# A spectral filter's weights in two buffers, loaded and stored at other places

## The chip, the cores and the metric

The kernel runs on one core of one Trainium2 chip, as one program. Its time is in device microseconds; the measure is the median of repeated runs. A profile is one more execution, recorded by the hardware: its span runs from the first to the last instruction of the program.

Five engines take part, each with its own queue, served in order: PE (TensorE, the matmuls), DVE (VectorE), ACT (ScalarE), POOL (GpSimd) and SP (SyncE, which here only issues DMAs). ACT and POOL issue a few DMAs too.

## The reference

The program computes a forward pass and all its gradients. The input x has 2048 rows of 448. Cut to what matters:

```python
def _A_ref(x, w_r, w_i):                       # w_r, w_i: 2048 x 225, the filter
    X = jnp.fft.rfft2(x.astype(jnp.float32), axes=(-2, -1))
    X = X * (w_r + 1j * w_i)
    return jnp.fft.irfft2(X, s=(S, D), axes=(-2, -1)).astype(jnp.bfloat16)

def _B_ref(x, w1, b1, w2, b2):
    h = _layernorm(x, axis=-1)
    u = _gelu(jnp.einsum("bsd,sf->bdf", h, w1) + b1)
    y = jnp.einsum("bdf,fs->bds", u, w2) + b2
    return y.transpose(0, 2, 1)

h  = x + _A_ref(_layernorm(x), w_r, w_i)
h2 = h + _B_ref(_layernorm(h), w1, b1, w2, b2)
# outputs: h2, and the gradients of x, w_r, w_i, w1, b1, w2, b2 for a given grad_out
```

The filter is read in the forward pass (X times W), read again in the backward pass (the gradient of x), and its gradient, of the same size, is an output. In bf16 the real and imaginary part are 0.92 MB each.

## The kernel before

**The transform.** The two-dimensional transform over 2048 x 448 is done as matmuls with small tables. The *first step* works by 16 tiles t of 128 rows: `row_a` multiplies a folded, normalized tile by the table `Rm` scaled with the rows' deviation, `row_b` by the table of the 448-point transform. The results of two tiles at a time are then moved by DMA to another arrangement of partitions, `D2`: these are the *row moves* (L697, at the end of `row_b`). Seven of eight go out on SP's queue, the last on ACT's. They are deferred by `RESH_LAG` in the program's order.

The *second step* (`s2_stage`, L704) takes `D2` in four sets s = 0 to 3 of four groups each: three small tables (`Vt`, `Ut`, `Un`) finish the forward transform of the set, `on_mult` multiplies by the filter on DVE, and three more tables begin the inverse transform. The result of each set is moved by DMA to `D3` (L740), by POOL, and of the last set by SP, POOL and ACT together. Then `inv_rows` (L765) finishes the inverse, tile by tile, with the row table `RTm` (made from `Rm` by one matmul in `gen_RT`, L525) and the table `csI`.

The forward pass and the backward pass both go through these steps; the backward `s2_stage` has `bwd_mult`, which multiplies by the filter's conjugate and then writes the filter's gradient over the filter, set by set.

**Work in the gaps.** PE runs other matmuls between these steps: `fill(n)` takes n pieces from a generator. In the forward pass it is `dg_gen` (L838), 14 x 16 matmuls of w2 transposed with grad_out, w2's tiles loaded by `load_w2T` (L303): the first five are turned on PE, the others come by a transposed DMA (L312). From the tenth tile on the loads are held back (`held_w2`) until the first step's end. In the backward pass `gw_gen` makes the gradients of w2 and w1, with transposed tiles from `st_load` (L1266) and `load_du` (L1252), and stores at L1372 and L1369.

**The filter.** One buffer `rW` holds it: 128 partitions, real and imaginary part (c), 16 groups (g), 225 columns. Partition 2q holds rows 16q and on in rising order, partition 2q + 1 rows in falling order, so a rising part is one run of 3600 elements in memory and a falling one is 16 runs of 225. `w_io` (L579) is a generator of 18 DMAs, either way: for each part four rising pieces of 16 partitions, four falling ones, and one for the row that is left over. `W_AT` says how many loads are issued at which tile of the first step (two at each of tiles 0 to 5, six at tile 6). The last four (rising, imaginary) go on POOL's queue, each behind a one-element memset on DVE that holds it back until DVE is there; the others go on SP's. For the gradient the same 18 moves go on SP in the last stage, at the tiles that `GW_AT` lists.

**Orders.** The instructions of PE, SP, DVE and ACT are issued in the order of the program text; POOL's are placed by a scheduler. SP's transfers take turns on eight semaphores, so each waits for the landing of the one eight before it. POOL also runs the Newton iterations (`newton_gp`, L407, lines L410 to L416) that give the deviation of each group of tiles; DVE scales `Rm` with it (`scale_R`, L621) and folds the tile (`fold_quarters`, L644) ahead of `row_a`.

The lines around the end of the first step that the change touches:

```python
    for _ in w_loads:
        pass
    ...
    turn_biases, place_biases = load_biases()
    cap[0] = NFB
    while held_w2:
        held_w2.pop(0)()
    fill(4)
    gen_RT()
    fill(7)
```

Of the kernel before, what the change touches and what calls it, by code (L numbers as in the profile page):

```python
# [17 lines left out]
P = 128  # L18
S = 2048
D = 448  # L20
DF = 225
KW = 226
# [3 lines left out]
NG = 16  # L26
# [98 lines left out]
def kernel(  # L125
# [20 lines left out]
    nc = tc.nc  # L146
# [99 lines left out]
    rS = region("rS", 7232)  # L246
    rO = region("rO", 3 * S)
    rX = region("rX", NG * 2 * KW)
    rW = region("rW", NG * 2 * KW)
    r452 = region("r452", 8 * 452)  # L250
    rAT = region("rAT", 2 * 4 * P)
    rst = region("rst", 2 * 7 * P)
# [320 lines left out]

    Wc = cut(rW, 0, 2, NG, DF)
    W = Wc.rearrange("p c g k -> p g c k")

    def w_io(dr, di, store):  # L579
        Wq = Wc.rearrange("(q s) c g k -> s q c g k", s=2)  # L580
        for c_, d in ((0, dr), (1, di)):
            moves = []
            for i in range(4):
                moves.append((Wq[0][16 * i:16 * i + 16, c_].rearrange("l g k -> l (g k)"), 16 * i, [[P * DF, 16], [1, 16 * DF]]))
                g0 = 0 if i else 1
                moves.append((Wq[1][16 * i:16 * i + 16, c_, g0:NG, :], P - 16 * i - g0,
                              [[P * DF, 16], [-DF, NG - g0], [1, DF]]))
            moves.append((Wq[1][0:16, c_, 0, :], 64, [[P * DF, 16], [1, DF]]))
            late = [m for n, m in enumerate(moves) if n in (0, 2, 4, 6)] if c_ and not store else []
            early = moves if not late else [m for n, m in enumerate(moves) if n not in (0, 2, 4, 6)]  # L590
            for n, (sb, row, dims) in enumerate(early + late):
                d_ap = bass.AP(d.tensor, d.offset + row * DF, dims)
                eng = nc.sync if n < len(early) else gp_
                if eng is gp_:
                    i = 32 * (n - len(early))
                    nc.vector.memset(Wc[i:i + 1, 1, 8, 0:1], 0.0)
                eng.dma_start(out=d_ap if store else sb, in_=sb if store else d_ap)
                yield

# [321 lines left out]
    GROUPS = {0: (6, 8), 1: (8, 10), 3: (10, 12), 5: (12, 14), 7: (14, 16)}  # L921
    STATS = {0: (6, 7), 1: (8, 9), **{t: (t + 8,) for t in range(2, 8)}}
    INV_S = {11: 0, 12: 1, 13: 2, 14: 3}
    W_AT = {**{t: 2 for t in range(6)}, 6: 6}
    FILL_A = (4, 4, 8, 12, 6, 3, 3, 4, 5, 3, 3, 2, 2, 2, 3, 3)
    FILL_B = (0, 0, 2, 2, 2, 2, 4, 4, 3, 2, 2, 2, 2, 2, 2, 2)
    def uv_step():
# [4 lines left out]
    for t in range(NT):  # L932
# [34 lines left out]
        if t in GROUPS:  # L967
            a, b = GROUPS[t]
            newton_gp(mvx[:, a:b, 1], rstd_x[:, a:b], slice(a, b))
        for _ in range(W_AT.get(t, 0)):  # L970
            next(w_loads, None)
        if t in INV_S:
# [6 lines left out]
        fill(FILL_B[t])  # L979
    for _ in uv:  # L980
        pass
    for _ in w_loads:
        pass
    gp_.memset(csF[:, 0, :, 0:1], 1.0)
    gen_inv_d(0)
    fill(6)
    gen_inv_d(1)
    turn_biases, place_biases = load_biases()
    cap[0] = NFB
    while held_w2:  # L990
        held_w2.pop(0)()
    fill(4)
    gen_RT()
    fill(7)

    def fwd_mult(s, j, x, y):
        w_mult(x, set_of(W, s)[:, 2 * j:2 * j + 2], y, False)
# [300 lines left out]

    def bwd_mult(s, j, xc, y):
        xs = set_of(Xs, s)[:, 2 * j:2 * j + 2, :, 0:DF]  # L1300
        gw = set_of(W, s)[:, 2 * j:2 * j + 2]
# [74 lines left out]
    for t in range(NT - LAG, NT + 4):  # L1376
        if t == 13:
            st_load(3)
        if t == NT - 2:
# [103 lines left out]
```

## Time and profile before

| What | Value |
|---|---|
| time, median of 3 runs | 340.99 us (340.43 to 341.34) |
| time of the profiled execution | 340.34 us |
| its span | 338.3 us |
| granted TensorE clock | 0.998 |
| first step, until the second starts | 0 to 48.4 us |
| forward second step, until `inv_rows` starts | 48.4 to 75.4 us |
| backward second step, until `inv_rows` starts | 238.7 to 288.9 us |
| last stage | 288.9 to 338.3 us |
| filter loads (L597): first to last issue | 11.5 to 37.9 us |
| filter gradient stores (L597): first to last issue | 289.2 to 320.6 us |
| row moves (L697): issue to landing, least, median, most | 2.3, 2.7, 3.7 us |
| moves behind the second step (L740): the same | 3.8, 5.5, 6.9 us |

How to read the views that follow. A *timeline* line gives start, length, engine, line, operation, what is written from what, how often, and in brackets how long the engine stood idle before it and what ended that. In the *chain of waits*, each line is start, length and what was then on the way to the end. In the view of *waits*, each line is who waited for whom, then total, times and the longest, in us. A transfer issued by SP, ACT or POOL is "DMA_DIRECT2D" or "DMA_TRANSPOSE"; SPq is SP's queue. Names of buffers are shown without their numbers, and `D2` and `D3` lie in the buffers shown as `r`. L84 is the helper through which DVE's and ACT's operations are issued; L220 and L225 are the helpers of the matmuls, L225 that of the small tables.

### The profile page before, as it was taken

What the parts mean: (1) busy time and instruction counts of PE and PEld (TensorE: products, weight loads), DVE (VectorE), ACT (ScalarE), POOL (GpSimd) and SP (SyncE); (2) the same over time, 40 slices, a digit from 0 to 9 for tenths busy, and PEclk for the clock granted to TensorE, in tenths of its full rate; (3) what the DMA queues carried; (4) which work ended last, traced back from release to release, by engine and by line L of the source; (5) the groups of instructions that cost most, each with busy time, mean ns of one, the idle gap of its engine ahead of it and who ended that gap; (6) DMA issues with size and microseconds to landing.
All of it is one profiled execution on the core that took longest, in us unless ns stands there. A gap on an engine that the chain in (4) does not pass through costs nothing.

```text
span 338.3 us, 7987 instructions
## 1 busy us (share of the span) xinstructions
PE 330.2 (98%) x2893; PEld 174.6 (52%) x2893; DVE 251.7 (74%) x670; ACT 206.7 (61%) x448; POOL 84.6 (25%) x254
## 2 busy tenths in 40 slices
PE   8999989999999999999999999999999999999995
PEld 4666554456545555555555555554344434555552
DVE  8998739827947888593227888786697993599994
ACT  6987666848965534423222346665588875588882
POOL 7767202412210000000001111210020222156670
PEclk9999999999999999999999999999999999999999
DMA  7999899959899999687877889837699999978885
GB/s 251 400 203 182 190 258 141 227 125 279 230 378 287 348 279 242 179 274 192 193 178 164 174 188 155 176 84 232 221 220 302 290 244 252 284 188 278 245 293 200
DMA packets 136198, 78.03 MB, mean 231 GB/s; under 512 B 86528, under 2 KB 127592, under 8 KB 136032
## 3 DMA queue, kind: packets, MB, share of 16 engines
q1 hardware_dynamic: 133288, 73.13, 84.5%
q0 software_dynamic: 2448, 3.83, 5.3%
q8 instruction: 22, 0.36, 0.5%
q10 hardware_dynamic: 424, 0.58, 0.5%
q14 instruction: 16, 0.13, 0.1%
HBM read 28.33 MB, written 22.04 MB: 149 GB/s over the span
## 4 chain that ended last, share of the span: by engine, by line
PE 83%; DVE 6%; DMA 4%; ACT 3%; issue 1%; POOL 1%; SPq 0%; DVEq 0%; ACTq 0%
PE ps_mm L220 68%; PE ps_ff L220 9%; PE ps_ff L225 3%; DMA r<-r 3%; ACT rO L84 2%; PE ps_mm L375 2%; DVE rS L84 2%; DVE r L84 1%; DMA r<-rX 1%; DVE rX L84 1%; DVE stats L84 1%; DVE rA L84 1%; ACT rE L84 1%; PE ps_mm L318 0%; DVE rG L84 0%
## 5 line engine op out<-in xcount | busy, mean ns | idle before, releaser
L220 PEld LDWEIGHTS <-r 128*128 128x128 bf16 (+2 forms) x628 | 58.6, 105 | 48.5 <-issue 3.0
L220 PEld LDWEIGHTS <-rS 128*128 128x128 bf16 (+1 forms) x468 | 36.2, 97 | 31.9 <-issue 6.0
L84 ACT CAST rO<-ps_mm 128x512 bf16<-128x512 f32 (+1 forms) x68 | 36.5, 584 | 14.5 <-PE ps_mm L220 11.9
L220 PE MATMUL ps_mm<-rD,r 128*128 128x448 bf16 x224 | 44.5, 352 | 0.0
L220 PEld LDWEIGHTS <-rst 128*128 128x128 bf16 (+1 forms) x320 | 23.9, 97 | 30.4 <-issue 12.1
L740 POOL DMA_DIRECT2D r<-r x29 | 17.4, 605 | 67.3 <-ACT r L84 56.7
L220 PE MATMUL ps_mm<-rC,rE 128*128 128x448 bf16 x144 | 32.1, 353 | 0.0
L220 PE MATMUL ps_mm<-rB,r 128*128 128x448 bf16 x160 | 31.2, 352 | 0.2 <-DVE rB L84 0.2
L220 PE MATMUL ps_mm<-rG,rst 128*128 128x512 bf16 (+1 forms) x128 | 28.5, 380 | 0.0
L220 PE MATMUL ps_mm<-r,rst 128*128 128x512 bf16 (+2 forms) x144 | 27.3, 345 | 0.0
L84 ACT ACTIVATE r<-ps_mm,rstd_h 128x448 bf16<-128x448 f32 x16 | 10.1, 634 | 26.8 <-PE ps_mm L220 26.8
L84 DVE SCALAR_TENSOR_TENSOR r<-ps_mm,b2col,r 128x448 bf16<-128x448 f32 x16 | 10.9, 682 | 19.9 <-PE ps_mm L220 18.6
L84 ACT ACTIVATE r<-rC 128x448 bf16<-128x448 bf16 x16 | 9.1, 570 | 26.7 <-DMA out_dram<-r 13.8
L84 ACT CAST r<-ps_ff 128x452 bf16<-128x452 f32 x43 | 23.1, 592 | 3.1 <-PE ps_ff L220 1.2
L1220 POOL TENSOR_SCALAR lcol<-lcol 128x1 f32<-128x1 f32 x16 | 8.5, 530 | 64.7 <-ACT r L84 64.7
L84 ACT ACTIVATE rG<-rG 128x896 bf16<-128x896 bf16 x14 | 13.3, 950 | 14.9 <-DVE rG L84 14.7
L220 PEld LDWEIGHTS <-rO 128*128 128x128 bf16 (+1 forms) x165 | 15.4, 98 | 12.3 <-ACT rO L84 0.2
L84 ACT CAST rS<-ps_ff 128x512 bf16<-128x512 f32 x31 | 18.0, 583 | 4.2 <-PE ps_ff L220 4.2
L220 PE MATMUL ps_ff<-csI,rAT 113*128 113x224 bf16 (+1 forms) x108 | 19.0, 298 | 0.2 <-DVE rA L84 0.2
L84 ACT CAST rG<-ps_mm 128x512 bf16<-128x512 f32 (+1 forms) x28 | 14.0, 539 | 7.6 <-PE ps_mm L220 7.5
L84 ACT CAST rAT<-ps_ff 113x512 bf16<-113x512 f32 x24 | 13.9, 586 | 7.7 <-PE ps_ff L220 7.5
L84 DVE TENSOR_SCALAR rG<-rG 128x896 bf16<-128x896 bf16 x28 | 10.9, 389 | 10.0 <-ACT rG L84 10.0
(200 smaller groups left out, 647.4 us busy)
## 6 DMA issues: line engine op xcount, KB each, us to landing
out_dram<-rO SPq DMA_DIRECT2D x34, 256.0 KB, 3.3
r<-in_B_w_dram SPq DMA_DIRECT2D x5, 1024.0 KB, 9.1
r<-r POOLq DMA_DIRECT2D x29, 113.0 KB, 5.5
out_dram<-rG SPq DMA_DIRECT2D x11, 256.0 KB, 3.1
r<-in_B_w_dram SPq DMA_DIRECT2D x3, 896.0 KB, 5.6
rS<-in_B_w_dram SPq DMA_DIRECT2D x3, 896.0 KB
rB<-in_B_w_dram SPq DMA_DIRECT2D x5, 512.0 KB, 8.1
r<-r SPq DMA_DIRECT2D x11, 226.0 KB, 2.5
```

The lines of the kernel that those rows point to most:

```text
L84: fn(**kw)
L220: nc.tensor.matmul(out, lhsT=lhsT, rhs=rhs, start=start, stop=stop)
L225: nc.tensor.matmul(out, lhsT=lhsT, rhs=rhs, start=start, stop=stop)
L375: nc.tensor.matmul(idle[:, 0:D], lhsT=rAT[:, 0:P], rhs=rAT[:, 0:D], start=True, stop=True)
L740: defer(RESH_LAG, lambda g=g, ab=ab, eng=eng: eng.dma_start(out=D3[rowbase(g):rowbase(g) + 29:4, :, :, :], in_=ab), ab)
L1220: gp_.tensor_scalar(out=m1, in0=ms, scalar1=-1.0 / D, scalar2=None, op0=ALU.mult)
```

## The change

The filter has two buffers of eight groups each, `rW[0]` for sets 0 and 1, `rW[1]` for sets 2 and 3, and `w_set(s)` picks a set. `w_io` goes through them one after the other. The four rising pieces of a part become one move of 64 partitions (4 blocks of 16 rows in memory, runs of 1800 elements); the falling pieces keep 16 partitions and have 8 groups, 7 in the piece beside the left-over row. That makes 12 moves for the first buffer and 10 for the second. On loading, the first four moves of the second buffer (falling, real) go on POOL's queue, behind one memset on DVE at tile 9.

The 12 loads of the first buffer are spread over tiles 0 to 8, POOL's four come at tile 9, and the other six are queued on SP behind the row moves: the two rising moves, then the first held w2 load, then the four falling moves, then the other held w2 loads. The loads of the biases are queued after these in the program text; in SP's order they stand behind the second held w2 load.

`gen_RT` is called behind `s2_stage` instead of ahead of it. The stores of the filter's gradient begin within the backward `s2_stage`: four after each of its passes 2, 3 and 4 (these are the first buffer's twelve), and the other ten at tiles 0 to 9 of the last stage.

```diff
-    rW = region("rW", NG * 2 * KW)
+    rW = [region(n, NG * DF) for n in ("rW0", "rW1")]
...
-    Wc = cut(rW, 0, 2, NG, DF)
-    W = Wc.rearrange("p c g k -> p g c k")
+    Wc = [cut(r, 0, 2, NG // 2, DF) for r in rW]
+
+    def w_set(s):
+        return Wc[s // 2].rearrange("p c (a b) k -> p b a c k", b=2)[:, s % 2]
 
     def w_io(dr, di, store):
-        Wq = Wc.rearrange("(q s) c g k -> s q c g k", s=2)
-        for c_, d in ((0, dr), (1, di)):
-            moves = []
-            for i in range(4):
-                moves.append((Wq[0][16 * i:16 * i + 16, c_].rearrange("l g k -> l (g k)"), 16 * i, [[P * DF, 16], [1, 16 * DF]]))
...
-            for n, (sb, row, dims) in enumerate(early + late):
+        H = NG // 2
+        for e in range(2):
+            Wq = Wc[e].rearrange("(q s) c g k -> s q c g k", s=2)
+            ups, dns = [], []
+            for c_, d in ((0, dr), (1, di)):
+                up, dn = Wq[0][:, c_], Wq[1][:, c_]
+                ups.append((d, up.rearrange("q g k -> q (g k)"), H * e, [[16 * DF, 4], [P * DF, 16], [1, H * DF]]))
+                for i in range(4):
+                    g0 = 0 if e or i else 1
+                    dns.append((d, dn[16 * i:16 * i + 16, g0:H], P - 16 * i - H * e - g0,
+                                [[P * DF, 16], [-DF, H - g0], [1, DF]]))
+                if not e:
+                    dns.append((d, dn[0:16, 0], 64, [[P * DF, 16], [1, DF]]))
+            moves = dns[:4] + ups + dns[4:] if e else ups[:1] + dns[:5] + ups[1:] + dns[5:]
+            for n, (d, sb, row, dims) in enumerate(moves):
+                eng = gp_ if e and n < 4 and not store else nc.sync
                 d_ap = bass.AP(d.tensor, d.offset + row * DF, dims)
...
-    W_AT = {**{t: 2 for t in range(6)}, 6: 6}
+    W_AT = {0: 2, 1: 1, 2: 2, 3: 1, 4: 2, **{t: 1 for t in range(5, 9)}, 9: 4}
...
+        if t == 9:
+            nc.vector.memset(Wc[1][:, 0, 0:2, 0:1], 0.0)
...
-    for _ in w_loads:
-        pass
...
-    turn_biases, place_biases = load_biases()
     cap[0] = NFB
+    for _ in range(2):
+        next(w_loads)
+    held_w2.pop(0)()
+    for _ in w_loads:
+        pass
     while held_w2:
         held_w2.pop(0)()
+    turn_biases, place_biases = load_biases()
     fill(4)
-    gen_RT()
     fill(7)
...
     s2_stage(lambda s: set_of(Xs, s), fwd_mult, 8, (8,) * 5, 0, split=True)
     sc.activation(out=warm, in_=eps_h, func=ACT.Sqrt)
+    gen_RT()
     fill(21)
...
+    g_out = w_io(out_2, out_3, True)
+
+    def store_gw(n):
+        for _ in range(n):
+            next(g_out)
...
-    s2_stage(lambda s: X_ring.next(), bwd_mult, 14, (14, 28, 14, 28, 20), N_FILL_B[4], {0: lambda: load_du(1), 1: lambda: (load_du(0), load_xall(0)), 2: lambda: load_xall(1), 3: lambda: load_du(2)},
+    s2_stage(lambda s: X_ring.next(), bwd_mult, 14, (14, 28, 14, 28, 20), N_FILL_B[4], {0: lambda: load_du(1), 1: lambda: (load_du(0), load_xall(0)), 2: lambda: (load_xall(1), store_gw(4)),
+              3: lambda: (load_du(2), store_gw(4)), 4: lambda: store_gw(4)},
              2.0 * INV_SD)
     Meter.slack = 2.0
-    g_out = w_io(out_2, out_3, True)
     X_AT = {0: 2, 4: 3}
-    GW_AT = tuple(range(12)) + tuple(range(1, 12, 2))
+    GW_AT = tuple(range(10))
```

More of the change, by code (lines that the diff above doesn't have):

```diff
@@ L572, in gen_inv_d @@
                         sc.activation(out=o, in_=i_, func=ACT.Copy, scale=f[0:KC])
-    Wc = cut(rW, 0, 2, NG, DF)
-    W = Wc.rearrange("p c g k -> p g c k")
+    Wc = [cut(r, 0, 2, NG // 2, DF) for r in rW]
+    def w_set(s):
+        return Wc[s // 2].rearrange("p c (a b) k -> p b a c k", b=2)[:, s % 2]
     def w_io(dr, di, store):
-        Wq = Wc.rearrange("(q s) c g k -> s q c g k", s=2)
-        for c_, d in ((0, dr), (1, di)):
-            moves = []
-            for i in range(4):
-                moves.append((Wq[0][16 * i:16 * i + 16, c_].rearrange("l g k -> l (g k)"), 16 * i, [[P * DF, 16], [1, 16 * DF]]))
[L585 to L590, printed above, removed]
-            for n, (sb, row, dims) in enumerate(early + late):
+        H = NG // 2
[14 more added lines that the diff above has]
+                eng = gp_ if e and n < 4 and not store else nc.sync
@@ L592, in w_io @@
                 d_ap = bass.AP(d.tensor, d.offset + row * DF, dims)
[L593 to L596, printed above, removed]
                 eng.dma_start(out=d_ap if store else sb, in_=sb if store else d_ap)
@@ L987 @@
     gen_inv_d(1)
-    turn_biases, place_biases = load_biases()
     cap[0] = NFB
+    for _ in range(2):
[3 more added lines that the diff above has]
+        pass
     while held_w2:
         held_w2.pop(0)()
+    turn_biases, place_biases = load_biases()
     fill(4)
-    gen_RT()
     fill(7)
     def fwd_mult(s, j, x, y):
-        w_mult(x, set_of(W, s)[:, 2 * j:2 * j + 2], y, False)
+        w_mult(x, w_set(s)[:, 2 * j:2 * j + 2], y, False)
     s2_stage(lambda s: set_of(Xs, s), fwd_mult, 8, (8,) * 5, 0, split=True)
     sc.activation(out=warm, in_=eps_h, func=ACT.Sqrt)
+    gen_RT()
     fill(21)
@@ L1300, in bwd_mult @@
         xs = set_of(Xs, s)[:, 2 * j:2 * j + 2, :, 0:DF]
-        gw = set_of(W, s)[:, 2 * j:2 * j + 2]
+        gw = w_set(s)[:, 2 * j:2 * j + 2]
         w_mult(xc, gw, y, True)
```

## The prediction

> **What bounds the kernel now.** I read the page first, then the waits, the timelines of the engines around every wait of TensorE, the chain of waits, and the queue of SyncE (SP).
>
> ```profile
> PE 330.2 (98%) x2893; PEld 174.6 (52%) x2893; DVE 251.7 (74%) x670; ACT 206.7 (61%) x448; POOL 84.6 (25%) x254
> ...
> DMA  7999899959899999687877889837699999978885
> ...
> q10 hardware_dynamic: 424, 0.58, 0.5%
> ```
>
> TensorE (PE) is busy 98% of the span, in program order, and the change leaves its matmuls as they are. So the change can win only what PE stands idle, and lose what it makes PE wait. The DMA row shows engines near full in most slices.
>
> ```profile
> PE ps_ff L225 <- DMA r<-rX: 0.9, 1, 0.9
> ...
> PE ps_ff L220 <- DMA r<-r: 0.7, 2, 0.5
> ...
> PE ps_ff L220 <- DVE rS L84: 0.7, 1, 0.7
> ```
>
> These are PE's largest waits behind its start: 0.91 us for a row move (L697) at the start of the second step, 0.49 and 0.24 for the moves behind the second steps (L740), 0.66 for a fold on VectorE. All PE waits after the start come to some 3.2 us, which is the ceiling of any gain. Two have causes that the diff touches. First the fold, by the timelines of POOL, DVE and PE:
>
> ```profile
> 28.34 0.20 POOL L413 TENSOR_TENSOR nt_f<-rstd_x 128x2 f32<-128x2 f32 x1
> 28.57 1.76 POOL L597 DMA_DIRECT2D rW<-in_A_w_i_dram  x3
> 30.34 0.24 POOL L414 TENSOR_TENSOR nt_f<-nt_f,mvx 128x2 f32<-128x2 f32 x1
> 30.54 0.53 POOL L597 DMA_DIRECT2D rW<-in_A_w_i_dram  x1
> ...
> 33.15 0.20 POOL L416 TENSOR_TENSOR rstd_x<-nt_f,rstd_x 128x2 f32<-128x2 f32 x1
> ```
>
> ```profile
> 33.38 0.25 DVE L84 TENSOR_SCALAR rX<-Rm,rstd_x 128x128 bf16<-128x128 bf16 x1 [0.81 <-POOL rstd_x L416]
> ...
> 36.20 0.32 DVE L84 TENSOR_SCALAR rX<-Rm,rstd_x 128x128 bf16<-128x128 bf16 x1 [0.78 <-POOL rstd_x L416]
> ```
>
> ```profile
> 35.02 0.40 PE L220 MATMUL ps_ff<-rX,rS 128*128 128x128 bf16 x4 [0.66 <-DVE rS L84]
> ```
>
> Four filter loads sit between the Newton operations on POOL and hold them for 1.76 + 0.53 = 2.29 us. DVE waits 0.81 us for the result, and PE 0.66 us for DVE. Now the start of the second step, by the chain, and SP's own timeline ahead of it:
>
> ```profile
> 43.01 1.23 DVE rX L84 x2
> 44.24 0.47 SPq L697
> 44.81 3.45 DMA r<-rX
> 48.40 0.72 PE ps_ff L225 x24
> ```
>
> ```profile
> 39.29 2.78 SPq L312 DMA_TRANSPOSE rO<-in_B_w_dram  x1
> 42.17 1.23 SPq L697 DMA_DIRECT2D r<-r  x2
> 43.50 1.85 SPq L697 DMA_DIRECT2D r<-rX  x3
> ```
>
> The last casts end at 44.24; SP, behind a long transposed load and five row moves, issues the last move only at 44.81, and it lands 3.45 us later. PE had come to the end of its fill at 48.40 - 0.91 = 47.49.
>
> **The change part by part.** Until the row moves SP issued 14 filter loads and POOL 4; now SP issues 12, of half the bytes (0.92 MB of 1.84), POOL issues 4 behind its last Newton operation, and 6 follow the last row move, with a transposed w2 load between them.
>
> *POOL.* The 2.29 us leave the Newton chain: its result at 33.35 would be there at 31.1, and DVE is ready for it at 32.57. So DVE's 0.81 go; its folds end at 34.96 - 0.81 = 34.15, before PE asks at 35.02 - 0.66 = 34.36. Gain for PE 0.66. The second wait (0.78) shrinks too and is worth the 0.06 that PE waits at 38.44. On POOL's queue the four new loads stand before a memset (needed at 43.94) and the first moves of L740 at 56.87; at 0.5 to 0.75 us each, from about 35 on, they are gone by 38. The four DVE memsets (59 ns each) become one. If the cover is gone, four loads of 0.6 us on POOL cost nobody anything before 43.9.
>
> *Row table.* One 128x128 matmul leaves the fill; the matmul behind it starts 0.05 us later now (45.94 to 45.99). Its cast (0.28 us at 47.87 on DVE) goes to ACT after the table load that ends at 72.77, and ACT is idle until 75.81; its reader starts at 75.37. Cover: 2 us of idle ACT; without it 0.3 us. Where it goes, PE has a wait of 0.49 that takes the 0.05. Gain before the step 0.05, cost 0.
>
> PE therefore reaches the end of its fill at 47.49 - 0.66 - 0.06 - 0.05 = 46.72.
>
> *Row moves.* They must have landed by then. The move on ACT's queue is issued at 44.30 and lands 3.66 us later; 0.72 earlier it lands at 47.24. SP's last one, if the queue is free when its casts end, goes out at 44.24 - 0.72 = 43.52 and lands by 46.97. Best bound: the moves land as fast as those in the second pass (2.3 to 2.5 us), and PE starts at 46.72, a gain of 1.68. Worst bound: SP's backlog stays, and the one small load now between the long transposed load and the moves adds its 0.61: 44.81 + 0.61 + 3.45 + 0.14 = 49.0, a loss of 0.6. SP now carries half the filter bytes through the stretch where the DMA row shows 9s, so I take the free queue: the step starts at 47.24, a **gain of 1.16**.
>
> *Second half of the filter.* Six loads are queued behind the row moves: two of 64 partitions (230 KB), the first held w2 transposed load, four of 58 KB, then the other transposed loads with three bias loads between. DVE reads sets 2 and 3 first at 59.47; issued by about 50 with landings of 5 to 7 us (median 6.5 of the loads on SP before), the loads are in by 57: cost 0, cover 2 us. The held w2 load was issued at 47.67, landed at 53.88, and PE's fill first reads it as the last of the 8 matmuls from 53.12, at 54.45: 0.57 us of cover. It is now issued about 2 us earlier (three bias loads, 45.45 to 47.58, are behind it, two filter loads of 0.6 before it), but its data stand behind 461 KB more. At the 283 GB/s of a busy stretch those take 1.6 us: it lands no later against PE than before. Taken 0; the other bound is a rival below. The later transposed loads have 2 to 5 us.
>
> *Early stores.* 18 stores between 289 and 321 become 12 within the backward second step and 10 behind it. They cost SP 12 x 0.6 = 7.4 us of issue from 261 to 285 and 0.92 MB, 3.3 us at 283 GB/s, in stretches whose DMA share is already 0.99 to 1.14. Behind them on SP wait transposed loads and output stores: the w1-gradient table issued at 272.62 landed 5.85 later and is read at 284.3, so 5.8 us of cover; output buffers come back at 293. Not covered is the last move of L740, on POOL's queue:
>
> ```profile
> 283.11 5.78 DMA r<-r
> ```
>
> PE waits 0.24 for it. Landings of this line range from 3.8 to 6.9 us. Bounds: -0.24 (its neighbours leave earlier) to +1.1 (6.9). The stretch at share 1.14 had 4.9 to 5.6, so I take 0. The eight stores taken from the last stage free SP there, and nothing waits for SP: 0.
>
> Sum: -1.16. The profiled execution took 340.34 us (span 338.3 and 2.04 around it), so 339.18; it lies 0.65 under the median of 340.99, the measure of the forecast: 340.99 - 1.16 = **339.8**.
>
> **The rivals.**
>
> *Given back.* The step starts early, but the w2 load or the last moves of L740 behind the step (0.49 wait now, at a queue that drains later) take it back, 0.5 to 1.1 us. For it: 0.57 us of cover; DMA share 1.1 to 1.2 from 48 to 70. Against: w2's earlier issue. Time 340.6.
>
> *Doesn't do what it says.* SP stays backlogged, row moves go out no earlier: +0.6, 341.6. For it: a transposed load holds SP 2.8 to 5.1 us whatever stands around it. Against: 0.92 MB less ahead.
>
> [...]
>
> [...]
>
> **How the numbers follow.** Forecast 0.42, given back 0.23, not what it says 0.10, few engines 0.25. A measurement of this kernel tells about 0.3% (1.0 us) from no change: faster 0.42, same 0.33, slower 0.25. The forecast's own range is 338.9 (340.99 - 1.68 - 0.24 and 0.2 of scatter) to 340.0. For 8 in 10 the range goes on through the two cases of no change into the middle of the slow one: 338.9 to 342.7.
>
> **What would show it.** PE's wait at the fold (35.02) gone; SP's last row move issued within 0.3 us of its casts' end; second step starting by 47.3; no PE wait in the fill at 53 to 54; PE's wait at 289 under 0.5. [...] The forecast is wrong if the step starts after 48 or if PE's waits after it grow by a microsecond.

## The result and the profile after

The changed kernel takes 352.97 us in the median of 6 runs (349.98 to 354.78), the kernel before 340.64 in 6 runs beside it (339.40 to 341.34). The ratio is 1.035, 95% interval 1.030 to 1.041: 12 us slower, where 1.2 us less was forecast. Where a kernel's executions fall into shorter and longer ones, ratios and intervals here are of the shorter ones alone. The profiled execution of the changed kernel is its fastest one: 349.98 us, span 348.0; so the profile shows 9.7 us of the loss, and the 3 us by which the median is longer stand in no profile.

| Point of the program | before, us | after, us | later by |
|---|---|---|---|
| forward second step starts | 48.40 | 46.70 | -1.70 |
| forward `inv_rows` starts | 75.37 | 81.52 | +6.15 |
| backward `inv_rows` starts | 288.93 | 298.66 | +9.73 |
| span | 338.3 | 348.0 | +9.7 |

So the early start came, larger than forecast; the forward second step then lost 7.85 us and the backward one 3.6; between and after them nothing changed. The waits of PE in the profile after (who waited for whom: total, times, longest, in us):

```profile
PE ps_mm L220 <- DMA rE<-in_B_w_dram: 4.4, 3, 2.5
PE ps_mm L220 <- DMA rO<-in_B_w_dram: 2.5, 1, 2.5
PE ps_mm L220 <- DMA rst<-rB: 2.1, 1, 2.1
...
PE ps_ff L225 <- DMA r<-rX: 0.3, 1, 0.3
PE ps_ff L220 <- DVE rS L84: 0.2, 1, 0.2
```

Of the two waits that the diff aimed at, the row move's fell from 0.9 to 0.3 and the fold's of 0.7 is gone (the 0.2 that is listed is another, at 22.05). In their place stand four waits on transposed w2 loads (rO, rE), 6.8 us together, and one of 2.1 us on the table of the w1 gradient. Where the w2 loads are late is seen on SP's own timeline, before and then after:

```profile
47.67 1.90 SPq L312 DMA_TRANSPOSE rO<-in_B_w_dram  x1
49.66 9.97 SPq L312 DMA_TRANSPOSE rE<-in_B_w_dram  x3
```

```profile
44.04 0.64 SPq L599 DMA_DIRECT2D rW<-in_A_w_r_dram  x1
44.73 0.60 SPq L599 DMA_DIRECT2D rW<-in_A_w_i_dram  x1
45.43 6.21 SPq L312 DMA_TRANSPOSE rO<-in_B_w_dram  x1
51.69 3.40 SPq L599 DMA_DIRECT2D rW<-in_A_w_i_dram  x4
55.19 1.93 SPq L312 DMA_TRANSPOSE rE<-in_B_w_dram  x1
```

The first held w2 load is issued 2.2 us earlier than before (45.43 for 47.67), but its issue lasts 6.21 us, for 1.90 before, and it lands at 55.23 instead of 53.88. SP stands for all that time, and the second w2 load, behind four more filter loads, is issued at 55.19 instead of 49.66. What the load stands for is seen in its packets of 256 bytes: from 49.5 to 51.0, while the filter's 3600-byte packets run, some 15 of them are open and 7 end; from 52.0 to 53.0 it is 20 open and 1134 ended. From there each load is late, as the chain of waits shows (start, length, what was on the way to the end):

```profile
45.43 9.75 DMA rO<-in_B_w_dram
55.19 5.84 DMA rE<-in_B_w_dram
...
63.23 10.05 DMA rE<-in_B_w_dram
...
73.33 0.36 PE ps_mm L220
```

The waits alone are not the whole loss. PE's busy time grew by 3.1 us (330.2 to 333.3) with the same 2893 matmuls. Stretches of the profile after (from:to, length, then per engine busy time and instructions, then the granted clock, DMA share and GB/s):

```profile
74.00:75.00 1.00, 1.00 (x45) 0.48 (x18) 0.60 (x2) 0.62 (x2) 0.00 (x0) 0.63 1.30 269
75.00:77.00 2.00, 2.00 (x7) 0.83 (x6) 0.56 (x2) 0.75 (x2) 0.60 (x1) 0.50 0.56 97
77.00:78.00 1.00, 1.00 (x6) 0.51 (x5) 0.00 (x0) 0.99 (x2) 0.00 (x0) 0.66 0.55 187
...
294.00:296.00 2.00, 2.00 (x8) 0.40 (x6) 0.00 (x0) 0.00 (x0) 0.00 (x0) 0.50 1.16 202
```

Behind the wait of 2.51 us that ends at 73.33 the clock is 0.5 for some 3.4 us, and again behind the wait of 2.09 us that ends at 292.71. Each costs half of that, about 1.7 us. The account closes: in the forward step 6.8 us of waits + 1.7 of clock - 0.5 (the wait at 75.37 that is gone) = 8.0, seen 7.85; in the backward step 2.1 + 1.7 - 0.2 = 3.6, seen 3.58. SP's timeline ahead of the table's wait, before and then after (the table is the last line of each):

```profile
269.34 3.19 SPq L1252 DMA_TRANSPOSE r<-rD  x1
272.62 2.21 SPq L1266 DMA_TRANSPOSE rst<-rB  x1
```

```profile
267.94 4.12 SPq L599 DMA_DIRECT2D out_dram<-rW  x4
...
277.61 5.34 SPq L1259 DMA_TRANSPOSE r<-rD  x1
283.00 2.55 SPq L599 DMA_DIRECT2D out_dram<-rW  x4
285.65 1.27 SPq L1273 DMA_TRANSPOSE rst<-rB  x1
```

### The profile page after: what moved, and what is told of

It reads as the page before. It is cut to its first block, busy times and chain, and to the rows that moved or that the text cites. A ratio compares the mean times of both kernels' runs of the same rounds, so it can differ in the third digit from the quotient of the medians.

```text
span 348.0 us, 7997 instructions
## 1 busy us (share of the span) xinstructions
PE 333.3 (96%) x2893; PEld 175.5 (50%) x2893; DVE 251.0 (72%) x666; ACT 206.7 (59%) x449; POOL 85.6 (25%) x254
## 4 chain that ended last, share of the span: by engine, by line
PE 81%; DMA 10%; DVE 4%; ACT 3%; issue 1%; POOL 0%; DVEq 0%; ACTq 0%
PE ps_mm L220 68%; PE ps_ff L220 8%; DMA rE<-in_B_w_dram 5%; DMA rO<-in_B_w_dram 3%; PE ps_ff L225 2%; DMA rst<-rB 2%; PE ps_mm L375 2%; ACT rO L84 2%; DVE r L84 1%; DMA r<-rX 1%; DVE stats L84 1%; DVE rA L84 1%; ACT rE L84 1%; DVE rX L84 0%; PE ps_mm L318 0%
## 5 line engine op out<-in xcount | busy, mean ns | idle before, releaser
L220 PE MATMUL ps_mm<-rC,rE 128*128 128x448 bf16 x144 | 34.2, 367 | 4.4 <-DMA rE<-in_B_w_dram 4.4
L220 PE MATMUL ps_mm<-r,rst 128*128 128x512 bf16 (+2 forms) x144 | 28.9, 358 | 2.1 <-DMA rst<-rB 2.1
L220 PEld LDWEIGHTS <-rE 128*128 128x128 bf16 x144 | 13.1, 101 | 15.8 <-DMA rE<-in_B_w_dram 5.7
L220 PE MATMUL ps_mm<-rC,rO 128*128 128x448 bf16 x80 | 18.1, 353 | 2.5 <-DMA rO<-in_B_w_dram 2.5
```

What stands on the lines that cost most here:

```text
L220: nc.tensor.matmul(out, lhsT=lhsT, rhs=rhs, start=start, stop=stop)
```

## The experiments

Two theories for the forward loss. *Few engines*: the 64-partition loads run on about four DMA engines, and a transposed load behind them waits for these. It is the author's guess: the trace of the changed kernel shows 3.7 of their packets open at a time in the mean, and says of no packet which engine moved it. *Queue*: it is the amount that stands on SP between the row moves and the w2 loads, in whatever shape. For the backward loss: the early stores make it, or it follows from the late forward pass. Runs of the kernel before beside each lay at 340.1 to 340.6 us (medians).

| Run | us | PE waits of note, us |
|---|---|---|
| w2_first | 349.0 (one) | step start 1.4; w2 1.8, 1.8; backward 1.6, 1.7 |
| w2_first_rise16 | 356.8 (one) | step start 1.7; w2 5.5; backward 7.7 |
| late_stores | 350.6 (one) | step start 2.0; w2 3.8; end 3.9 |
| before_pool9 | 346.7 (one) | step start 1.7; 3.5 without a cause shown |
| all_ahead | 351.6 | Vt 5.5; 1.7 without a cause shown; backward 4.5 |
| all_ahead_late | 347.7 | Vt 3.3; 1.7 without a cause shown; end 0.7 |
| ups_ahead | 355.8 | Vt 9.8; backward 4.1 |
| stores_ups_late | 349.5 | w2 5.9; backward 2.6 |
| all_sp | 352.8 | step start 5.8; backward 1.4; last stage 3.4 |
| all_sp_late | 350.5 | step start 6.2; last stage 2.4 |
| before_sp18 | 342.8 | step start 0.6; last move behind the step 1.0 |
| before_pool4 | 341.1 | step start 0.5; last move behind the step 1.1 |
| half64, again | 345.1 (346.7) | w2 1.7, 3.2; backward 1.7 (w2 5.9) |
| half16 | 340.1 | step start 1.8; 0.8 without a cause shown |
| bwd_only | 352.9 | 7.5 for a buffer; 1.5 |
| bwd_pass4 | 344.3 | backward 1.2; last stage 2.5 |

**w2_first.** The w2 load ahead of the two 64-partition loads.

```diff
-    for _ in range(2):
-        next(w_loads)
     held_w2.pop(0)()
```

> The changed kernel with one order turned: the first held w2 load goes out ahead of the two 64-partition filter loads instead of behind them; all bytes and shapes stay. Theory (the 64-partition loads run on about four DMA engines, and a transposed load behind them waits for these): the first w2 load lands about 6 us after its issue, near 50.5 instead of 55.2, PE's wait of 2.46 us at 55.28 is gone; the two filter loads still take 5 to 6 us at about 4 packets at once, and the later w2 loads keep part of their waits (together 1 to 3 of 4.4 us); time 344 to 348. Rival (it is the amount queued on SP behind the row moves, in whatever order): the first wait goes, but the next w2 loads land as late as they do now, near 61, 67 and 73, and PE's waits of the step stay above 5 us; time within 1.5 us of 350.

349.0 us. SP's timeline of this run:

```profile
45.07 3.13 SPq L312 DMA_TRANSPOSE rO<-in_B_w_dram  x1
48.26 0.63 SPq L599 DMA_DIRECT2D rW<-in_A_w_r_dram  x1
48.94 3.35 SPq L599 DMA_DIRECT2D rW<-in_A_w_i_dram  x5
52.39 5.14 SPq L312 DMA_TRANSPOSE rE<-in_B_w_dram  x1
```

The first w2 load is issued in 3.13 us and PE does not wait for it. The long issue has moved to the next one, which now stands behind the two loads (5.14), and with it the wait (1.79 at 61.09). The two loads' 128 packets of 3600 bytes take 6.8 us here. In the changed kernel they run from 45.5 to 51.4 with 3.7 at a time in the mean: 461 KB in 5.9 us, 78 GB/s over the whole and some 95 in its steady part. That the first load's wait follows the place is what few engines said; the 3.6 us of w2 waits that are left lie above its bound of 3 and under the rival's 5, and the time, of one execution, is where the rival had it. A long issue alone proves no shape: the kernel before has one of 5.12 us at 32.09, with four filter loads of 16 partitions on POOL's queue just ahead of it and no 64-partition load anywhere.

**w2_first_rise16.** As before it, with four loads of 16 partitions for each of the two.

```diff
-                ups.append((d, up.rearrange("q g k -> q (g k)"), H * e, [[16 * DF, 4], [P * DF, 16], [1, H * DF]]))
+                    ups.append([(d, up[16 * i:16 * i + 16], 16 * i + H * e, [[P * DF, 16], [1, H * DF]]) for i in range(4)])
```

> As the run with the w2 load first, and each of the second half's two 64-partition loads is made as four loads of 16 partitions, the shape of the kernel before: the same bytes, eight issues for two (3.6 us more on SP). Theory (few engines): the 3600-byte packets are through in 2 to 3 us, with 8 or more at once, and PE's waits on w2 in the step are under 1 us together; time 342 to 345. Rival (amount and queue on SP): eight issues make SP later, and the waits on w2 are as large as with the 64-partition loads or larger; time 347 to 351.

356.84: the theory's number missed by 12 us. SP's timeline:

```profile
45.45 2.49 SPq L312 DMA_TRANSPOSE rO<-in_B_w_dram  x1
47.99 3.06 SPq L604 DMA_DIRECT2D rW<-in_A_w_r_dram  x4
51.10 5.88 SPq L604 DMA_DIRECT2D rW<-in_A_w_i_dram  x8
57.08 2.85 SPq L312 DMA_TRANSPOSE rE<-in_B_w_dram  x1
```

Behind 16-partition loads a w2 load is issued in 2.85 us, not 5.14, so the shape does here what few engines says. But each 58 KB now costs 0.63 us of SP, some 91 GB/s, and the 3600-byte packets take 6.2 us in all: issuing takes as long as the two loads of 64 partitions took. The second w2 load leaves 4.7 us later than in the run above, and PE waits 5.5 us for it. Both theories hold a part here: the shape blocks, and so does the number of issues.

**late_stores.** All 22 stores in the last stage.

```diff
-    ... 2: lambda: (load_xall(1), store_gw(4)), 3: lambda: (load_du(2), store_gw(4)), 4: lambda: store_gw(4)},
+    ... 2: lambda: load_xall(1), 3: lambda: load_du(2)},
-    GW_AT = tuple(range(10))
+    GW_AT = tuple(range(12)) + tuple(range(1, 11))
```

> The changed kernel without the early stores: all 22 stores of the filter's gradient go in the last stage, two a tile, none in the backward second step. Theory (the stores, four of them just ahead of the table's transposed load, make this land late): PE's wait of 2.09 us for that table is gone or under 0.5, and with it the stretch of granted clock 0.5 behind it (1.3 us of PE time); time 3 to 3.5 us under the changed kernel's, and the last stage gives none of it back. Rival (the table is late because SP is behind since the forward step, or the last stage then waits for its output stores): the wait stays at 1.5 to 2.5 us, or the time stays within 1 us of the changed kernel's. The forward step keeps its 6.8 us of waits in both.

350.63. No wait over 0.2 us from 250 to 320: the backward loss is gone. In its place PE waits at the end:

```profile
PE ps_mm L220 <- DVE rG L84: 3.9, 1, 3.9
```

In the last stage DVE stood up to 3.9 us for stores to free its output buffers. The second branch of the rival: the stores' cost has moved. The forward part is that of the changed kernel, and shows it a second time: step start 47.58, w2 waits 3.8 us.

**before_pool9.** POOL's release alone, in the kernel before.

```diff
-    W_AT = {**{t: 2 for t in range(6)}, 6: 6}
+    W_AT = {**{t: 2 for t in range(6)}, 6: 2, 9: 4}
```

> The kernel before with one part of the change alone: the four filter loads on POOL's queue are released at tile 9, behind its last Newton iteration, instead of at tile 6. Theory (this part gave the early start of the second step): the waits of DVE for the deviation (0.81 and 0.78 us) go, PE's wait of 0.66 us at the fold too, and the second step starts 0.7 to 1.7 us earlier, at 46.7 to 47.7; no new wait follows; time 0.7 to 1.7 us under the kernel before. Rival (the row moves on SP's full queue decide the start): the fold's wait goes, but the step starts within 0.3 us of 48.4 and the time is the same.

346.69 in one execution, wrong for both. The fold's wait went, but POOL's loads, issued from 35.70 to 37.93, ran beside a transposed load (36.69) and landed at up to 46.12, and the row moves took 5.9 to 6.9 us instead of 2.7 (median): the step started at 49.22. A further 3.51 us that end at 69.45 are a wait for which the profile shows no cause (see the open points below).

**all_ahead, all_ahead_late, ups_ahead, stores_ups_late.** The second half, or only its 64-partition loads, ahead of the row moves; early or late stores; and only the two early 64-partition stores made late. The diff is all_ahead's.

```diff
+            if e and not store:
+                moves = ups + dns[4:] + dns[:4]
...
-    W_AT = {0: 2, 1: 1, 2: 2, 3: 1, 4: 2, **{t: 1 for t in range(5, 9)}, 9: 4}
+    W_AT = {**{t: 2 for t in range(9)}, 9: 4}
...
-    for _ in range(2):
-        next(w_loads)
-    held_w2.pop(0)()
-    for _ in w_loads:
-        pass
```

> The changed kernel with the second half of the filter loaded ahead of the row moves too: 18 loads on SP at tiles 0 to 8, two a tile, POOL's four at tile 9, nothing behind the row moves but the w2 loads and the biases. Buffers, shapes and the early stores stay. Theory A (what was lost in the second step is that filter loads stand between the row moves and the w2 loads): the first w2 load leaves SP by 45 and lands by 51, PE's waits on w2 in the step fall from 6.8 us to under 1.5, inv_rows starts by 77.5 instead of 81.5; the row moves land no earlier than in the kernel before, the step starts at 47 to 49.5; time 344 to 347, the rest being the backward loss. Rival B (the 64-partition shape is what costs, wherever it stands): the row moves or the w2 loads, which share the same few engines with these loads, land late, the step starts after 49.5 or PE waits over 3 us in it; time 348 or more.

> As the run with the whole filter loaded ahead, and the 22 stores of the gradient in the last stage, none in the backward second step. If the early stores alone make the backward loss (2.1 us of wait, 1.3 of granted clock): no wait over 0.5 us in the backward second step, no dip of the clock there. If then the last stage can take the 22 stores: time 340 to 342. Rival (22 stores in the last stage hold SP 2.4 us longer than 18, and the last outputs wait): PE waits 2 to 4 us for an output buffer at the end, as in the run with late stores alone, time 343 to 346.

> The changed kernel with only the two 64-partition loads of the second half moved ahead of the row moves (tiles 7 and 8); the four falling loads of 16 partitions stay behind the row moves, and the first held w2 load goes between. Few engines: no w2 load stands behind a 64-partition load any more, so each is issued in 2 to 3.5 us instead of 6.2, the first lands by 51, and PE's waits on w2 are 1 to 3 us together instead of 6.8; the falling loads move 450-byte packets at 26 to 35 ns and hold nothing. Rival (any filter load behind the row moves costs the same): the w2 loads behind the four falling ones are as late as now (61, 67, 73), waits over 4 us. [...]

> The changed kernel, forward part untouched, with the two 64-partition stores of the first buffer taken out of the backward second step and put into the last stage; its ten 16-partition stores stay early (0.46 of 0.92 MB). Few engines: the transposed table that PE waited 2.09 us for lands within 5.5 us of its issue, PE's wait for it is under 0.5 us, and no granted clock of 0.5 follows; time 2 to 3.5 us under the changed kernel. Rival (the number of stores ahead of the table on SP): the wait stays at 1.5 us or more, as SP has the same four stores just ahead of it.

In the first three a new wait came that neither theory had: DVE's memset at tile 9, which holds POOL's loads back, writes a place of the buffer that a 64-partition load now writes before it, so DVE stood (up to 10.8 us idle before the scaling of `Rm` and the memset), and PE 3.3 to 9.8 us for `Vt`. That DVE stood for that load is read from the program, the profile names no cause; the all_sp runs below have no memset and no such wait. Their times, 351.6 (1.023 to 1.038 times before), 347.7 (1.016 to 1.028) and 355.8 (1.040 to 1.051), are no measure of the order. What they do show: with no 64-partition load between the row moves and the w2 loads PE had no wait for w2 at all, where the changed kernel had 6.8 us.

stores_ups_late took 349.46 (1.021 to 1.032). The table's wait is gone, as few engines said, and the time is at the end of what was expected. But the backward loss is not gone with it: from one `inv_rows` to the other it takes 215.97 us (213.56 before, 217.14 in the changed kernel), for PE now waits 2.65 us for the last move behind the second step, with the clock halved behind it. Beside the changed kernel's profile the forward part, which this run leaves as it was, ends 2.4 us earlier, the backward step takes 1.2 less, and the last stage, where the halved clock now falls, 2.7 more.

```profile
PE ps_ff L220 <- DMA r<-r: 2.6, 1, 2.6
```

**all_sp, all_sp_late.** All 22 loads on SP at tiles 0 to 10, the 64-partition loads of the second half first, without the memset; early or late stores. Two places of the diff:

```diff
-                eng = gp_ if e and n < 4 and not store else nc.sync
+                eng = nc.sync
...
-    W_AT = {0: 2, 1: 1, 2: 2, 3: 1, 4: 2, **{t: 1 for t in range(5, 9)}, 9: 4}
+    W_AT = {t: 2 for t in range(11)}
```

> The changed kernel with all 22 filter loads on SP at tiles 0 to 10, two a tile, nothing of the filter on POOL and no memset on DVE; nothing of the filter behind the row moves. Buffers, 64-partition shapes and early stores stay. Theory (place behind the row moves makes the forward loss): no wait of PE for Vt; waits on w2 in the step under 1 us together; step starts 47 to 49, inv_rows at 75 to 77 (81.5 in the changed kernel, 75.4 before). The backward loss stays: 2 to 5 us of PE waits from 285 to 300; time 343 to 347. Rival (the shape of 64 partitions makes it, wherever it stands): the row moves or the w2 loads land late all the same, inv_rows after 78.5; time over 348.

> As the run with all loads on SP, with all 22 stores of the gradient in the last stage. The pair differs in the early stores alone. Theory (early stores cost 2 to 5 us in the backward step): 2 to 4 us under its partner, no wait over 0.5 us from 250 to 300; time 340 to 343. Rival (the backward loss follows from the forward lateness, or the last stage takes it back): within 1 us of its partner.

352.79 (1.030 to 1.042) and 350.49 (1.027 to 1.033), both over the theory's numbers. Again no wait for w2 in either, though all_sp's first w2 load also leaves 2.6 us ahead of the step's start, for 1.3 in the changed kernel and 0.7 before. But the step starts at 52.91 and 53.54, after 5.8 and 6.2 us of waiting for the row moves. SP's timeline in all_sp:

```profile
33.94 0.60 SPq L601 DMA_DIRECT2D rW<-in_A_w_r_dram  x1
34.59 0.57 SPq L601 DMA_DIRECT2D rW<-in_A_w_i_dram  x1
...
37.40 5.44 SPq L312 DMA_TRANSPOSE rO<-in_B_w_dram  x1
42.88 1.27 SPq L601 DMA_DIRECT2D rW<-in_A_w_r_dram  x2
...
44.88 2.54 SPq L601 DMA_DIRECT2D rW<-in_A_w_i_dram  x4
...
48.21 1.98 SPq L701 DMA_DIRECT2D r<-rX  x3
```

The transposed load behind the two 64-partition loads (33.94, 34.59) holds SP 5.44 us, and the last four row moves leave at 47.5 to 50.2. So the place behind the row moves makes the w2 loads late, and ahead of them the same loads make the row moves late. The rival's number came, its "wherever it stands" in part: the last row move leaves 4.8 us later than in before_sp18 below, 2.2 of it by the longer issue of the transposed load, 2.6 by four loads more on SP. The pair differs by 2.3 us for the early stores, at the low end of what was expected: backward waits of 1.4 us are gone, and the last stage waits 2.4 instead of 3.4.

**before_sp18, before_pool4.** The kernel before with POOL's four loads on SP, or on POOL at tile 4.

```diff
-            late = [m for n, m in enumerate(moves) if n in (0, 2, 4, 6)] if c_ and not store else []
+            late = []
```

> The kernel before with POOL's four filter loads given to SP: 18 loads at tiles 0 to 8, two a tile, in the shapes of before; POOL's Newton iterations are free of loads. If the release of POOL is worth what the first step of the changed kernel showed: the fold's wait of 0.66 us is gone, the step starts 0.5 to 1.7 us earlier, time 339.0 to 340.3 against 340.3 to 340.9 for before. Rival (SP's queue, four loads longer, holds the row moves): the step starts after 48.4 and the time is 0 to 3 us longer.

> The kernel before with POOL's four filter loads released at tile 4 instead of 6 (their place in the list of loads moved ahead of the other imaginary ones): they stand between other Newton operations, and their data come earlier, farther from the row moves. If the collision of these loads with the transposed load and the row moves made the run with POOL's loads at tile 9 slow: row moves here land no later than in the kernel before (step starts by 48.4), and the time is within 1 us of it. If any shift of these loads does it: over 342.

342.78 (1.001 to 1.008) and 341.05 (0.998 to 1.005): neither beats the kernel before. In before_sp18 the transposed load at the same place as in all_sp (37.56), behind 16-partition loads, is issued in 3.24 us, the last row move leaves SP at 44.86 and the step starts at 47.80.

**half64, half16.** The shape, in the kernel before: 230 KB of the filter directly ahead of the first held w2 load, as one load of 64 partitions or as two of 16 (115 KB each). The other half stays on POOL, as four loads or two; the partner with two starts the second step no earlier (48.62, for 47.75 in half64).

```diff
+                behind = [(Wq[0][:, 1, 8:16].rearrange("q g k -> q (g k)"), 8, [[16 * DF, 4], [P * DF, 16], [1, 8 * DF]])]
...
+            behind, late = late[2:], late[:2]
```

> The kernel before, in which one half of the rising imaginary part (groups 8 to 15, 230 KB) is loaded behind the row moves, directly ahead of the first held w2 load, as one load of 64 partitions; POOL loads the other half in its old place; the biases stand behind the second w2 load. To be set against the run with the same bytes in two loads of 16 partitions. Few engines: its 64 packets of 3600 bytes take 2.5 to 3 us, some 4 at a time; the w2 load's issue lasts 4 us or more and its 256-byte packets come behind those; it lands 1 to 2.5 us later, counted from the issue of the filter load, than in the partner, and PE waits 0.5 to 2 us for it. Rival (only bytes and issues count): the w2 load lands within 0.5 us of the partner's, counted the same way, or earlier by the issue saved.

> The partner: the kernel before, in which 230 KB of the rising imaginary part (the pieces 2 and 3 of POOL's four, all 16 groups) are loaded behind the row moves as two loads of 16 partitions, directly ahead of the first held w2 load; POOL loads the other two; biases as in the partner. Few engines: the packets are through in under 1.5 us, more than 8 at a time, the w2 load's issue lasts 2 to 3.3 us, PE waits under 0.5 us for w2. Rival: as the partner, plus 0.6 us for the second issue.

> The same kernel as the run half64 (230 KB behind the row moves as one load of 64 partitions), profiled once more, as its first profile fell on one of its longest executions. Few engines: the 3600-byte packets go at about 4 at once and 90 to 100 GB/s, the w2 load's issue behind them lasts 4.5 us or more against 3.1 in the partner, and the w2 loads after it are issued 1 to 2 us later than the partner's, into the moves behind the step; PE waits 1 us or more for one of them. Rival: all w2 loads are issued and land within 0.6 us of the partner's.

345.05 (340.88 to 352.92; 1.004 to 1.015) and 340.13 (338.53 to 345.00; 0.994 to 1.002): by its interval the one load of 64 partitions costs 1.3 to 5 us, and the 16-partition form costs nothing. half64 scatters widely, and its profiles, of 347.36 and 346.71 us, both lie above its median, so what an execution of 341 us does is not shown. SP's timelines, half16 first, then half64 again:

```profile
44.31 1.88 SPq L598 DMA_DIRECT2D rW<-in_A_w_i_dram  x2
46.29 3.10 SPq L312 DMA_TRANSPOSE rO<-in_B_w_dram  x1
49.48 1.91 SPq L312 DMA_TRANSPOSE rE<-in_B_w_dram  x1
...
58.61 4.13 SPq L312 DMA_TRANSPOSE rO<-in_B_w_dram  x1
```

```profile
44.33 0.70 SPq L601 DMA_DIRECT2D rW<-in_A_w_i_dram  x1
45.14 4.86 SPq L312 DMA_TRANSPOSE rO<-in_B_w_dram  x1
50.09 3.15 SPq L312 DMA_TRANSPOSE rE<-in_B_w_dram  x1
...
61.51 6.73 SPq L312 DMA_TRANSPOSE rO<-in_B_w_dram  x1
```

The first w2 load is not late for PE in either (its issue ends at 50.00 and 49.39), so the wait of 0.5 to 2 us that few engines set for it did not come. The second starts 0.6 us later in half64, the fifth 2.9 later, and it then lies among the moves behind the second step (L740) and lands 8 us later than the partner's (69.26), where PE waits for it, on PE's timeline of half64 again:

```profile
77.56 2.80 PE L220 MATMUL ps_mm<-rC,rO 128*128 128x448 bf16 x7 [5.91 <-DMA rO<-in_B_w_dram]
```

Stretches of half64 again show the rates (DMA share and GB/s are the last two columns):

```profile
44.00:46.00 2.00, 2.00 (x15) 1.19 (x14) 0.24 (x1) 0.97 (x5) 0.06 (x1) 1.00 1.05 383
47.00:50.00 3.00, 2.68 (x58) 1.32 (x57) 1.02 (x5) 1.80 (x5) 0.00 (x0) 1.00 1.05 114
50.00:52.00 2.00, 2.00 (x27) 0.90 (x41) 1.71 (x3) 0.59 (x2) 0.00 (x0) 1.00 1.11 250
...
60.00:64.00 4.00, 4.00 (x80) 1.93 (x70) 3.21 (x8) 3.50 (x9) 2.36 (x4) 1.00 1.11 100
67.00:72.00 5.00, 4.65 (x69) 2.16 (x66) 1.30 (x4) 2.36 (x4) 1.64 (x3) 1.00 1.21 135
```

383 GB/s with row moves alone; 114 while the 64-partition load runs and the w2 load waits behind it; 250 with the w2 load by itself; 100 and 135 where w2 loads run beside POOL's moves. The DMA share is over 1 in all five, whatever was moved. So the rival's "within 0.6 us" held for the first w2 load, and few engines' "later ones into the moves behind the step" for the rest.

**bwd_only, bwd_pass4.** The forward pass and the buffer of the kernel before; the changed kernel's stores, as they were or all twelve behind pass 4.

```diff
+    ... 2: lambda: (load_xall(1), store_gw(4)), 3: lambda: (load_du(2), store_gw(4)), 4: lambda: store_gw(4)},
...
+    ... 2: lambda: load_xall(1), 3: lambda: load_du(2), 4: lambda: store_gw(12)},
```

> The kernel before with the stores of the changed kernel alone: its forward pass as it was, one buffer, 12 of 22 stores in the backward second step after its passes 2, 3 and 4. Theory (the early stores make a loss of their own): PE waits 1.5 to 5 us between 278 and 292 for a transposed table, a transposed gradient tile or a move behind the step, with a stretch of granted clock 0.5 where a wait is over 2 us; time 342.5 to 347. Rival (the backward waits of the changed kernel came from its late forward pass): waits there under 0.5 us, time within 1 us of before.

> As the run with the early stores alone, with all 12 of them after pass 4, behind the transposed loads of passes 2 and 3 on SP. If it is their place ahead of the transposed loads on SP that costs: the waits of PE between 278 and 292 are under 0.6 us, time within 1 us of before. If it is their bytes beside the moves of POOL, wherever in the step: a wait of 1 us or more for the last moves behind the step at 289, time 341.5 to 345.

bwd_only took 352.92 (1.029 to 1.044), far over both numbers, for a cause of its own. SP and DVE in this run:

```profile
260.46 0.45 SPq L1289 DMA_DIRECT2D rE<-in_A_x_dram  x1
270.02 3.56 SPq L615 DMA_DIRECT2D out_dram<-rW  x4
```

```profile
279.65 0.70 DVE L84 TENSOR_TENSOR rW<-rS 128x450 bf16<-128x450 bf16 x2 [6.10 <-DMA out_dram<-rW]
```

In one buffer the first store stands on SP until DVE has written parts of the next set, and DVE then stands for the stores. The parts don't overlap; the program's order of reads and writes in one buffer makes them wait. That is what the change's two buffers are for, and it makes this run no measure of the early stores.

bwd_pass4 has none of that: 344.32 (1.004 to 1.018). The transposed loads go out as in the kernel before (the table at 272.48, for 272.62), PE has no wait for them, and what is left is 1.22 us for the last move behind the step at 289.01 and 2.5 us in the last stage. So their place ahead of the transposed loads on SP makes the table late; and with the place mended, the wait and the time that were set for the stores' bytes came. These two waits, 3.7 us together, are most of what the run lies above the kernel before (344.32 for 340.14). That the stores' bytes are behind them is argued, not shown.

## Why the prediction was wrong

*POOL and the row moves: right, and at the best bound.* The fold's wait fell from 0.66 to under 0.1 (the 0.2 that is left is another, at 22.05), SP's last row move left at 42.76, just as the last casts (begun at 42.02, 0.74 us long) ended, and the step began at 46.70; "best bound" said 46.72. The near hit is in part luck: PE was through with its fill at 46.43, 0.3 earlier than worked out, and then stood 0.27 for a row move. The choice of the middle, 47.24, cost 0.5 us. before_pool9 speaks against this gain being POOL's alone: in the kernel before the same release made the start later.

*Second half of the filter: this step failed.* It said of the w2 load: "it lands no later against PE than before. Taken 0". It landed at 55.23, and PE waited 2.46 us. The sum had set 461 KB at 283 GB/s, 1.6 us; they took 5.9 us, 3.7 packets at a time in the mean, and the transposed load's issue behind them stood on SP for 6.21 us.

*"The later transposed loads have 2 to 5 us": failed too, and cost more.* What the working left out is SP: a load whose issue lasts 6.21 us instead of 1.9 holds everything behind it, and the four falling loads add 3.4. The second w2 load left 5.5 us later, and three later ones cost 0.94, 0.91 and 2.51 us. half64 shows the same growth from 0.6 us to 8.

*Early stores: failed at "5.8 us of cover".* The working counted their issue, 7.4 us, and their bytes, but set no part of either against the table, which stands behind eight of them on SP. Eight stores took 4.1 + 2.6 us there, and a transposed load between them 5.34 instead of 3.19; the table left at 285.65, which is 6.9 us later than before when the forward delay of 6.15 is taken off, and PE waited 2.09 us. In stores_ups_late eight stores of 16 partitions stand there; by the same account the table leaves 4.2 us later, and PE does not wait, so the 64-partition stores add the part that is felt. bwd_pass4 puts the stores behind the table, and this wait is gone; in the three runs with all stores late no backward wait is over 0.7 us. The move of L740, "taken 0" with +1.1 as its bound, made no wait in the changed kernel, where PE came late, and 1.2 in bwd_pass4 and 2.6 in stores_ups_late.

*Not in the working at all: the clock.* Each of the two waits over 2 us that were followed by half the clock cost 1.7 us more.

*The rivals.* The result is in the slow case, which had 0.25 under the name "few engines", and 10 us above the end of the range, 342.7, that was put in the middle of this case. No run shows that the 64-partition loads run on four engines; what the changed kernel showed is 3.7 of their packets open at a time in the mean, a transposed load behind them that is issued in 6.21 us (5.14 in w2_first), and with that four waits for w2, 6.8 us together. That shape alone is not the whole cause is shown by w2_first_rise16: in loads of 16 partitions, as many bytes behind the row moves block by their issues.

Still open: the waits of 0.8 to 3.5 us near 66 to 72 in before_pool9, all_ahead, all_ahead_late and half16, for which the profile names no cause. The traces show this beside them: in all four PE stands ahead of the same one, the 1722nd of the matmuls and weight loads that the profile lists, and it goes on 1.3 to 1.5 us after a packet of 16 KB on the queue that the profile calls "instruction" (in before_pool9 it runs from 66.41 to 67.99, and PE goes on at 69.45). In none of the other profiles does this instruction start less than 1.3 us after such a packet. No run varied it, so it is not shown to be the cause. Open too is why w2 loads and POOL's moves together reach only 100 to 135 GB/s. No version here beats the kernel before; half16 equals it.

## What to carry to other kernels

What a transfer cost on the queue here was how long it held the queue (6.21 us for one load, 1.90 before), not its bytes over the best rate: read from a trace how many of its packets run at once, and look at the issue length of the transposed load behind it. When a load with little cover is delayed, follow the whole train behind it to the place where it meets other traffic, for there, in half64, a delay of half a microsecond grew to eight. Merging transfers saves issues and need not save time: here 461 KB took 5.9 us as two loads of 64 partitions, and 6.2 us as eight of 16 whose issues came one by one. How much was split decided: 230 KB as two loads of 16 partitions cost nothing where one of 64 cost 1.3 to 5 us.

## What the runs showed of the hardware

**The granted clock after a wait.** Over the profiles of the changed kernel and the experiments, PE waits of 1.3 to 1.8 us in the middle of the kernel were never followed by a lower clock (15 of them), those of 1.97 to 2.65 us in 4 of 7 cases, and those of 3.2 us and more always (14 of 14). Behind the wait the clock is 0.5 for another 3.1 to 5.8 us, of which half is lost. So the wait of 2.09 us in the changed kernel cost 3.8 us with the 1.7 of the clock, and no lower clock followed its wait of 2.46 us.

What decides between them is not shown. In the changed kernel the clock is 0.5 from 74.27 to 77.68 and from 292.72 to 296.13, 3.41 us each time. Of the 3.41 us that end with the wait PE was busy 0.90 us at the wait of 2.51 us, which ends at 73.33, and 0.95 at the wait of 2.46 us, which ends at 55.28: the clock fell behind the first, 0.94 us after its end, and stayed behind the other.

**The DMA share is no throughput here.** It stood at 1.05 at 383 GB/s and at 1.11 at 100 GB/s (half64 again, 44 to 46 and 60 to 64). The 9s of the DMA row, read in the prediction as engines near full, therefore say little about the room that is left.
